# Scores of twelve later attention units computed in the first six steps of a fused top-k attention and MLP kernel

## The chip, the cores and the metric

The kernel runs on one core of one Trainium2 chip. The metric is the device time of the program in microseconds (us). All data are 32-bit floats. The core's engines run side by side, each with an instruction queue of its own that it works off in order: TensorE (PE; its weight loads are shown apart as PEld), VectorE (DVE), ScalarE (ACT), GpSimd (POOL) and SyncE (SP), which issues the DMAs here.

## The reference, cut to what matters

```python
def _attn_ref(q, k, v):                       # (8, 8, 576, 64) each
    scores = scale * np.matmul(q, k.transpose(0, 1, 3, 2))
    kth = np.partition(scores, -32, axis=-1)[..., -32:-31]
    scores = np.where(scores >= kth, scores, -1e9)
    attn = np.exp(scores - np.max(scores, axis=-1, keepdims=True))
    attn = attn / (np.sum(attn, axis=-1, keepdims=True) + 1e-09)
    return np.matmul(attn, v)

x = attn_out.transpose(0, 2, 1, 3).reshape(4608, 512)
h = x @ w_in                                  # 512 x 2048
out = np.maximum(0.01 * h, h) @ w_out         # 2048 x 512
```

For each query only its 32 largest scores of 576 stay in the softmax. The output of the eight heads, side by side, then goes through a two-layer MLP with a leaky ReLU.

## The kernel before, in words

**Units.** The 64 (batch, head) combinations are taken as 32 pairs of heads; a pair's q and k lie in tiles of 128 partitions (64 for each head) by 576. A *unit* is 128 query rows of one pair (two heads), or 64 rows of each of two pairs where 576 leaves a remainder. There are 144 units, 18 to a batch: 16 whole and 2 left ones, the left ones first in odd batches.

**A step of the loop (L540) per unit.** The order of all instructions is written out by hand in this loop. Step `s` touches several units at once:

- `top_k` of unit `s` (`cur`) on VectorE: a maximum and a minimum of the two halves (L251), then four rounds of MAX8 (L256) and MATCH_REPLACE8 (L259).
- `mask` of unit `s-1` (`old`) on GpSimd (L269, L270), its exponentials and their sums on ScalarE (`exponents` L273, `sums` L278, which writes `ze`).
- of unit `s-2` (`older`): the reciprocal `rz` on VectorE (L282), the normalization on ScalarE (L285), and the transposition. ScalarE splits each 32-bit word in two halves (L294), SP writes them to DRAM (L295), and a transposing DMA brings them back as the tile `wT` (L299). Units 14, 15, 23 and 31 (`HASTY`) are transposed on TensorE instead.
- `values` of a pair of units whose `wT` has come (L336, TensorE), kept in `x` by ScalarE (`keep_values` L350). For units from 14 on this happens at the end of the even step three after the pair's odd unit, for units 15, 23 and 31 (`HURRIED`) one step sooner. Earlier units take place `MIDDLE`, one step later.
- in every even step, at its end, `scores` of units `s+2` and `s+3`: eight matmuls (L220) into one `narrow` and two `wide` PSUM tiles, then four ScalarE copies (L227) to the tiles `s_sb` (five buffers). The first two units are scored before the loop by `first_scores` (L236, L242), whose shape is two halves of 288 keys for each head.

**The MLP** works on chunks of tokens: two of 128, then seventeen of 256. A chunk becomes ready when the last of its units is in `x`. Its matmuls (`ph` L392, ScalarE's activation into `gT` L398, `pz` L404, copy L413, store L414) are cut into pieces, which `mlp_steps` places between the pieces of attention at seven slots a step. `slot_budget` spreads the work in hand evenly up to the step in which the next chunk becomes ready.

**Before the loop** the two weight matrices come in 16 pieces as 64-bit numbers in the `raw` tiles (three buffers) and are rounded to 32 bits on VectorE, ScalarE, GpSimd and TensorE (`round_weights`).

**Loads.** `load_qk` (L161) issues q and k of a pair on SP, one after the other; five pairs lie in `loads` tiles, and the last three of each round of eight pairs in a `raw` tile. `load_more` runs at the end of each step; a pair's tiles are loaded anew 8 steps after the last unit that uses them. `load_v` does the same for v. SP takes all DMAs in the order of the program: a transfer that has to wait holds those behind it.

**Constants.** `EARLY_SHARE` is the MLP budget of a slot while only the first two chunks are in hand. `HURRY` is 20: before it, normalization is placed later in the step.

## Time and profile before

| quantity | value |
|---|---|
| time of three runs | 1466.9, 1467.38, 1470.24 us; median 1467.38 |
| the profiled execution's own time | 1466.93 us |
| its span | 1465.2 us, granted TensorE clock 0.98 of full |
| TensorE matmul busy | 1395.2 us (95%) |
| VectorE busy | 1320.3 us (90%) |
| ScalarE, GpSimd busy | 1100.4 and 1097.0 us (75% each) |
| a step of VectorE with no wait in it | 8.87 us on the mean of two (17.7 us for a pair of steps) |
| first `top_k` starts | 60.9 us |
| DMAs | 222.30 MB, 152 GB/s over the span |
| landing of a DMA after its issue, median | 2.1 us for 288 KB of `split`, 3.2 and 3.7 us for q and k (288 KB), 6.7 us for 1024 KB of weights |

How to read it: the page of the profile gives the busy time of each engine and 40 equal slices of the span; a digit is the busy share of one slice (36.6 us) in tenths. The chain of waits goes back from the last instruction, at each step to what released it. In a timeline or a group list, the square bracket or the last column gives the idle time of the engine just before an instruction, and who ended it. A record such as `L220 ... x8` counts matmul records, and a 32-bit matmul leaves two of them. Idle time of an engine that is not the bound costs nothing.

### The profile page before, as it was taken

Reading aid. Unit: us, or ns where it says so; the run is one execution under the profiler, and the core shown is the slowest. Engines: PE = TensorE matmul, PEld = TensorE weight load, DVE = VectorE, ACT = ScalarE, POOL = GpSimd, SP = SyncE. Lnnn points to the kernel's source line nnn. Section 1 sums busy time; section 2 is a strip of 40 time slices with the busy share of each in tenths; the row PEclk is TensorE's granted clock in tenths of the full one; section 3 lists DMA queues with packets and bytes.
Section 4 is the critical chain, followed back from the end, with each engine's and each line's share of the span. In section 5 each row is a group of like instructions: output and inputs, shape, how many; then the busy total and the mean of one; then the engine's idle time right before and its main releaser. Section 6 shows DMA issues by size and latency. Waiting matters only on the chain.

```text
span 1465.2 us, 24106 instructions
## 1 busy us (share of the span) xinstructions
PE 1395.2 (95%) x8066; PEld 927.8 (63%) x8068; DVE 1320.3 (90%) x3401; ACT 1100.4 (75%) x1984; POOL 1097.0 (75%) x744
## 2 busy tenths in 40 slices
PE   7617999999999999999999999999999999999999
PEld 2314548575757676767676767666666666666674
DVE  7999999999999999999999999999999999999600
ACT  8658878777887777777777777777777777777710
POOL 3388888878888888787878888878788878787700
PEclk9957999999999999999999999999999999999999
DMA  9834534654366455665567545655467555664510
GB/s 329 304 85 133 146 105 116 171 154 136 107 196 185 129 137 155 171 185 137 146 168 193 141 138 132 194 174 148 128 167 202 136 140 144 155 141 132 148 45 14
DMA packets 388940, 222.30 MB, mean 152 GB/s; under 512 B 333904, under 2 KB 333904, under 8 KB 386896
## 3 DMA queue, kind: packets, MB, share of 16 engines
q1 hardware_dynamic: 388816, 220.77, 53.7%
q8 instruction: 63, 1.03, 0.3%
q14 instruction: 61, 0.50, 0.1%
HBM read 46.14 MB, written 92.01 MB: 94 GB/s over the span
## 4 chain that ended last, share of the span: by engine, by line
PE 81%; DVE 16%; ACT 1%; issue 1%; DMA 0%; POOL 0%; DVEq 0%; SPq 0%; ACTq 0%; POOLq 0%
PE pz L404 31%; PE ph L392 30%; PE wide L336 10%; DVE tops L256 6%; PE wide L220 6%; DVE pairs L259 5%; PE narrow L220 3%; DVE pairs L251 2%; DVE w_out L155 1%; DVE scale L152 1%; DVE w_in L155 1%; DMA raw<-in_weights_dram 0%; DVE top L133 0%; DVE scale L131 0%; ACT s_sb L285 0%
## 5 line engine op out<-in xcount | busy, mean ns | idle before, releaser
L269 POOL TENSOR_SCALAR pen<-s_sb,tops 128x576 f32<-128x576 f32 x288 | 637.7, 2214 | 208.7 <-DVE tops L256 144.5
L256 DVE MAX8 tops<-pairs 128x8 f32<-128x288 f32 (+1 forms) x1152 | 635.9, 591 | 0.0
L404 PE MATMUL pz<-w_out,gT 128*128 128x512 f32 x1152 | 505.1, 595 | 2.4 <-ACT scale L365 2.4
L392 PE MATMUL ph<-x,w_in 128*128 128x256 f32 x2176 | 482.9, 381 | 0.9 <-ACT gT L398 0.9
L259 DVE MATCH_REPLACE8 pairs<-tops,pairs 128x288 f32<-128x288 f32 (+1 forms) x864 | 460.2, 538 | 0.0
L392 PEld LDWEIGHTS ph<-x,w_in 128*128 128x128 f32 x2176 | 409.4, 190 | 77.7 <-issue 22.2
L270 POOL TENSOR_TENSOR s_sb<-s_sb,pen 128x576 f32<-128x576 f32 x288 | 406.6, 1412 | 24.0
L404 PEld LDWEIGHTS pz<-w_out,gT 128*128 128x128 f32 x1152 | 216.4, 190 | 267.2 <-issue 262.5
L294 ACT COPY split<-s_sb 128x1152 uint16<-128x1152 uint16 x280 | 309.4, 1146 | 0.0
L285 ACT ACTIVATE s_sb<-s_sb,rz 128x576 f32<-128x576 f32 x288 | 207.6, 773 | 43.4 <-DVE rz L282 43.4
L273 ACT ACTIVATE s_sb<-s_sb,nbias 128x576 f32<-128x576 f32 x288 | 222.3, 772 | 12.8 <-POOL s_sb L270 12.8
L251 DVE TENSOR_TENSOR pairs<-s_sb 128x576 f32<-128x576 f32 x288 | 213.5, 780 | 9.9
L336 PEld LDWEIGHTS wide<-wT,vt 128*64 128x64 f32 x3200 | 161.7, 139 | 65.1 <-issue 34.6
L336 PE MATMUL wide<-wT,vt 128*64 128x128 f32 (+1 forms) x3200 | 179.1, 268 | 22.4 <-ACT s_sb L227 21.1
L398 ACT ACTIVATE gT<-ph 128x512 f32<-128x512 f32 x136 | 80.7, 593 | 56.3 <-PE ph L392 55.6
L227 ACT COPY s_sb<-wide 128x704 f32<-128x704 f32 x142 | 107.2, 755 | 21.0 <-PE wide L220 21.0
L350 ACT COPY x<-wide 128x128 f32<-128x128 f32 (+1 forms) x160 | 32.2, 260 | 112.5 <-PE wide L336 112.4
L220 PE MATMUL wide<-kt,qt 64*128 64x352 f32 (+1 forms) x392 | 76.4, 503 | 26.0 <-ACT s_sb L227 23.0
L413 ACT COPY o_sb<-pz 128x512 f32<-128x512 f32 x36 | 21.1, 586 | 98.0 <-PE pz L404 98.0
L227 ACT COPY s_sb<-narrow 128x448 f32<-128x448 f32 x142 | 68.7, 537 | 1.2 <-PE narrow L220 0.6
L282 DVE RECIPROCAL rz<-ze 128x2 f32<-128x2 f32 x144 | 22.3, 155 | 45.9 <-ACT ze L278 45.8
L259 DVE MATCH_VALUE_LOAD pairs<-tops,pairs 128x8 f32 x864 | 62.6, 72 | 0.0
(61 smaller groups left out, 623.2 us busy)
## 6 DMA issues: line engine op xcount, KB each, us to landing
apart<-split SPq DMA_DIRECT2D x280, 288.0 KB, 2.1
raw<-in_weights_dram SPq DMA_DIRECT2D x15, 1024.0 KB, 6.7
vt<-in_vk_dram SPq DMA_DIRECT2D x32, 320.0 KB, 3.4
out_dram<-o_sb SPq DMA_DIRECT2D x36, 256.0 KB, 2.6
qt<-in_qT_dram SPq DMA_DIRECT2D x20, 288.0 KB, 3.2
kt<-in_kT_dram SPq DMA_DIRECT2D x20, 288.0 KB, 3.7
raw<-in_qT_dram SPq DMA_DIRECT2D x12, 288.0 KB, 3.2
raw<-in_kT_dram SPq DMA_DIRECT2D x12, 288.0 KB, 3.6
```

Of the source, the lines that this page charges most:

```text
L220: nc.tensor.matmul(to[r0:r0 + u.rows, i, :], qt[d, u.q0:u.q0 + u.rows], kt[d, k0:k1], start=True, stop=True)
L251: nc.vector.tensor_tensor(pairs[:, :, n, :], u.both[:, :, 0:HS], u.both[:, :, HS:S], op)
L256: nc.vector.max(out=u.tops[:, i, r, :], in_=rest[i])
L259: nc.vector.match_replace(out=rest[i], in_to_replace=u.tops[:, i, r, :], in_values=rest[i], imm_value=LOWEST)
L269: nc.gpsimd.tensor_scalar(pen, u.s[i], u.tops[:, i, ROUNDS - 1, 7:8], MASKED, ALU.is_lt, ALU.mult)
L270: nc.gpsimd.tensor_tensor(u.s[i], u.s[i], pen, ALU.add)
L273: nc.scalar.activation(u.s[i], u.s[i], AF.Exp, bias=u.nbias[:, i:i + 1], scale=SCALE, accum_out=u.z[:, i:i + 1])
L285: nc.scalar.activation(u.s[i], u.s[i], AF.Copy, bias=0.0, scale=u.rz[:, i:i + 1])
L294: nc.scalar.copy(split, pairs[:, :, h])
L336: nc.tensor.matmul(po[side * D:(side + 1) * D, o, :], vt[:, c, side, :], u.wT[:, c + side * NKC if c + 1 < NKC else c, r:r + n], start=(c ...
L392: nc.tensor.matmul(ph[:, i, 0:n], w_in[c][:, f * P:(f + 1) * P], x[c][:, 0:n], start=(c == 0), stop=(c == HP - 1),)
L404: nc.tensor.matmul(pz[0:m, 0:DMODEL], gT[:, f, r0:r0 + m], w_out[f // 4][:, f % 4, :], start=(f == 0), stop=(f == NFC - 1),)
```

## The change

Twelve units, namely 24, 25, 32, 33, 40, 41, 48, 49, 56, 57, 64 and 65, are no longer scored two steps ahead of their use, in the groups at the ends of steps 22, 30, 38, 46, 54 and 62. Instead:

- Before the loop, `load_early` brings k (whole) and q (128 columns for each unit) of the two pairs concerned into each of the three `raw` tiles.
- At the ends of steps 0 to 5, `score_early` scores 4, 2, 1, 2, 1 and 2 of the units with `keep_scores`, in the shape of `first_scores`. ScalarE copies the scores into one of three parts of `gT`, which the MLP does not use yet, and SP stores them to a DRAM tile `kept`.
- Three steps ahead of its use, each unit's scores are fetched from `kept` into its `s_sb` tile (`fetch_scores`), on SP right after the step's transposing DMA.
- q and k of the later pairs are put on a list `waiting`, and one tensor of it is issued in a step, in the same place after the transposing DMA, when no fetch takes that place. The three pairs whose q and k lie in `raw` tiles in the first round are loaded at the end of step 5 instead of step 0.
- The `at_once` condition takes `HASTY` in place of `HURRIED`, which adds step 16.

```diff
--- before.py
+++ after.py
@@ -63,6 +63,7 @@
     work = ctx.enter_context(tc.tile_pool(name="work", bufs=2))
     small = ctx.enter_context(tc.tile_pool(name="small", bufs=5))
     halves = ctx.enter_context(tc.tile_pool(name="halves", bufs=3, space=bass.MemoryType.DRAM))
+    kept = ctx.enter_context(tc.tile_pool(name="kept", bufs=1, space=bass.MemoryType.DRAM))
     ps_sc = ctx.enter_context(tc.tile_pool(name="ps_sc", bufs=1, space=bass.MemoryType.PSUM))
     ps_ml = ctx.enter_context(tc.tile_pool(name="ps_ml", bufs=2, space=bass.MemoryType.PSUM))
 
@@ -158,16 +159,20 @@
 
     qk_of, v_of = {}, {}
 
-    def load_qk(pi):
+    def load_qk(pi, at_once=True):
         if pi % (LOADED + 3) < LOADED:
             qt = loads.tile([P, S], F32, name="qt")
             kt = loads.tile([P, S], F32, name="kt")
         else:
             raw = raws.tile([P, WCH, 4], U16, name="raw").rearrange("p n w -> p (n w)").bitcast(F32)
             qt, kt = raw[:, 0:S], raw[:, S:2 * S]
-        nc.sync.dma_start(qt, qT[pi])
-        nc.sync.dma_start(kt, kT[pi])
+        waiting.extend([(qt, qT[pi]), (kt, kT[pi])])
         qk_of[pi] = qt, kt
+        if at_once:
+            while waiting:
+                nc.sync.dma_start(*waiting.pop(0))
+
+    waiting = []
 
     def load_v(pi):
         v_of[pi] = loads.tile([P, NKC, 2, D], F32, name="vt", bufs=LOADED_V)
@@ -240,6 +245,46 @@
         u.s = [u.both[:, i, :] for i in range(2)]
         for i in range(2):
             nc.scalar.copy(u.s[i].rearrange("p (h n) -> p h n", h=2), ps[i][:, :, 0:HS])
+
+    early_of = {}
+
+    def load_early(us):
+
+        raw = raws.tile([P, WCH, 4], U16, name="raw").rearrange("p n w -> p (n w)").bitcast(F32)
+        at = 0
+        for pi in sorted({u.pairs[0] for u in us}):
+            kt = raw[:, at:at + S]
+            nc.sync.dma_start(kt, kT[pi])
+            at += S
+            for u in us:
+                if u.pairs[0] == pi:
+                    early_of[u] = raw[:, at:at + P], kt
+                    nc.sync.dma_start(early_of[u][0], qT[pi][:, u.q0:u.q0 + P])
+                    at += P
+
+    kept_of = {}
+
+    def keep_scores(u):
+
+        k = len(kept_of)
+        qt, kt = early_of.pop(u)
+        ps = [ps_sc.tile([P, 2, 512], F32, name="wide", bufs=2) if (2 * k + i) % 3 else
+              ps_sc.tile([P, 2, 512], F32, name="narrow") for i in range(2)]
+        for half in range(2):
+            for i, _, side, _ in u.parts:
+                d = slice(side * D, (side + 1) * D)
+                nc.tensor.matmul(ps[i][:, half, 0:HS], qt[d, :], kt[d, half * HS:(half + 1) * HS],
+                                 start=True, stop=True)
+        both = gT.rearrange("p f n -> p (f n)")[:, k % 3 * 2 * S:(k % 3 + 1) * 2 * S]
+        for i in range(2):
+            nc.scalar.copy(both[:, i * S:(i + 1) * S].rearrange("p (h n) -> p h n", h=2), ps[i][:, :, 0:HS])
+        kept_of[u] = kept.tile([P, 2 * S], F32, name=f"kept{k}")
+        nc.sync.dma_start(kept_of[u], both)
+
+    def fetch_scores(u):
+        u.both = work.tile([P, 2, S], F32, name="s_sb", bufs=5)
+        u.s = [u.both[:, i, :] for i in range(2)]
+        nc.sync.dma_start(u.both.rearrange("p i n -> p (i n)"), kept_of[u])
 
     def top_k(u):
 
@@ -455,6 +500,9 @@
 
     steps = units
 
+    KEPT = (24, 40, 56)
+    EARLY_SCORES = {0: 4, 1: 2, 2: 1, 3: 2, 4: 1, 5: 2}
+
     def unit(n):
         return steps[n] if 0 <= n < len(steps) else None
 
@@ -486,12 +534,31 @@
     with tc.manual_schedule():
         last = {p: n for n, u in enumerate(steps) for p in u.pairs}
 
+        to_keep = [[steps[n] for n in (a, a + 1, a + 8, a + 9)] for a in KEPT]
+        early_units = {u for us in to_keep for u in us}
+        to_load, to_keep = list(to_keep), [u for us in to_keep for u in us]
+        assert all(len(u.pairs) == 1 for u in to_keep)
+
+        def score_early(count):
+
+            for _ in range(min(count, len(to_keep))):
+                keep_scores(to_keep.pop(0))
+                if len(to_keep) % 4 == 0 and to_load:
+                    load_early(to_load.pop(0))
+
         def load_more(s):
 
             for of, load, n, lag in ((v_of, load_v, LOADED_V, LAG + 1), (qk_of, load_qk, LOADED + 3, 8)):
+                if of is qk_of and to_keep:
+                    while len(of) < LOADED:
+                        load(len(of))
+                    continue
                 while len(of) < NPAIR and (len(of) < n or last[len(of) - n] + lag <= s):
-                    load(len(of))
-                    if lag > LAG + 1 and len(of) > n:
+                    if of is v_of or len(of) < n:
+                        load(len(of))
+                    else:
+                        if not waiting:
+                            load(len(of), at_once=False)
                         break
 
 
@@ -513,6 +580,8 @@
                     pass
             if n:
                 load_weights(n + 2)
+            if n >= len(jobs) - 2:
+                load_early(to_load.pop(0))
             if 0 <= n - len(jobs) + HP + 1 < HP:
                 load_qk(n - len(jobs) + HP + 1)
 
@@ -538,6 +607,7 @@
             attended(*place)
 
         for s in range(len(steps) + LAG + 1):
+            assert s < 7 or not to_keep
             cur, old, older, new = unit(s), unit(s - 1), unit(s - 2), ()
             if s % 2 == 0:
                 new = [u for u in steps[s + 2:s + 4] if u]
@@ -559,7 +629,7 @@
                 weights_of(older)
             mlp_steps(budget)
             weighed = values(s, MIDDLE)
-            at_once = s - 2 in HURRIED or any(at == (s, MIDDLE) for at, _ in ready_at)
+            at_once = s - 2 in HASTY or any(at == (s, MIDDLE) for at, _ in ready_at)
             if at_once:
                 keep(weighed, s, MIDDLE)
             slot()
@@ -575,6 +645,10 @@
                 keep_transposed(older) if s - 2 in HASTY else transpose(older, lambda: mlp_steps(budget))
             if not older or s - 2 in HASTY:
                 mlp_steps(budget)
+            if unit(s + 3) in early_units:
+                fetch_scores(unit(s + 3))
+            elif waiting:
+                nc.sync.dma_start(*waiting.pop(0))
             slot()
             slot()
             mlp_steps(budget)
@@ -584,11 +658,14 @@
             mlp_steps(budget)
             if not at_once:
                 keep(weighed, s, MIDDLE)
+            if new and new[0] in early_units:
+                new = ()
             if new and s < HURRY:
                 scores(new)
             keep(values(s, END), s, END)
             if new and s >= HURRY:
                 scores(new)
+            score_early(EARLY_SCORES.get(s, 0))
             budget = slot_budget(s + 1)
             mlp_steps(budget)
             load_more(s)
```

## The prediction, made before the changed kernel was run

> **What bounds the kernel now.** I read the page first (busy shares, slices, chain), then sums over stretches, then the chain in pieces, then each engine's waits over the same stretches, then the timelines. The page, its shares and three slice rows:
>
> ```profile
> PE 1395.2 (95%) x8066; PEld 927.8 (63%) x8068; DVE 1320.3 (90%) x3401; ACT 1100.4 (75%) x1984; POOL 1097.0 (75%) x744
> ...
> PE   7617999999999999999999999999999999999999
> DVE  7999999999999999999999999999999999999600
> ...
> PEclk9957999999999999999999999999999999999999
> ```
>
> TensorE is full from about the sixth slice to the last, VectorE from the second to about 1380 us. The two change places as the bound, and the early TensorE is idle at half clock. Sums over stretches (start:end, length, then busy us of PE, PEld, DVE, ACT, POOL, clock, DMA share, GB/s):
>
> ```profile
> 60.90:113.90 53.00, 15.04 (x104) 10.76 (x100) 52.56 (x137) 29.70 (x52) 38.13 (x27) 0.61 0.38 110
> ...
> 253.00:387.00 134.00, 133.98 (x780) 88.78 (x779) 126.69 (x330) 101.81 (x192) 106.80 (x73) 1.00 0.51 142
> 387.00:462.00 75.00, 74.80 (x418) 50.49 (x417) 74.44 (x199) 59.84 (x111) 63.78 (x43) 1.00 0.66 187
> 462.00:640.00 178.00, 177.16 (x1143) 124.61 (x1144) 172.27 (x446) 142.11 (x264) 145.47 (x99) 1.00 0.56 153
> 640.00:1403.00 763.00, 762.97 (x4466) 516.95 (x4465) 707.26 (x1843) 594.70 (x1087) 605.60 (x404) 1.00 0.57 154
> ```
>
> In the first row (steps 0 to 5) TensorE does 15 us in 53: 38 us are free there, and 23 of ScalarE. VectorE sets the pace; its waits over 61 to 190 us are empty. Over 190 to 387 us it waits 6.5 us in six places, over 387 to 505 nothing, over 505 to 650 us 4.6, then 26.7 up to 1370 us. All are of one kind, the reciprocal waiting for ScalarE's `ze`, which stands in ScalarE's queue behind work that waits for TensorE. So VectorE's waits measure how late TensorE is. The chain of waits says the same: VectorE 61 to 190 us, TensorE 192 to 384, VectorE 384 to 462, TensorE from there to the end. Two places of it:
>
> ```profile
> 305.48 0.79 PE wide L220 x4
> 306.27 0.76 PE narrow L220 x8
> 307.03 0.59 PE wide L220 x4
> ...
> 460.76 0.08 DVE rz L282
> ...
> 461.55 0.76 ACT s_sb L285
> 462.31 0.49 ACT gT L398
> ...
> 462.85 1.99 PE ph L392 x8
> ```
>
> First: a score group of two units costs TensorE 0.79+0.76+0.59 = 2.14 us on the path. Second: at 462 us TensorE waits for VectorE (through ScalarE's queue), so work taken from it shortly before is lost there.
>
> **What the Trainium skill says.** "TensorE: Matmul & The Clock Gate", section "What's actually happening": the idle array runs at half clock. Agrees: values (L336 x40) take 4.45 to 4.53 us at 107 and 125 us, 2.33 on the later chain. "DMA: Bandwidth & Descriptors", section "Queues, rings and completion order": descriptors of one ring start in order. No run here shows a fetch ahead of a split; the loads L168/L169, issued at 461.62 and 462.25 us right after a transposing transfer, are the nearest thing.
>
> **The change, part by part.**
>
> *Removed.* The groups at the ends of steps 22, 30, 38, 46, 54 and 62 leave TensorE and ScalarE; only their eight matmuls and four copies are missing from either queue, nothing else changes places there. TensorE: 6 x 2.14 = 12.8 us. What each is worth depends on who is late. They ran at 268, 343, 415, 486, 560 and 634 us.
> - 268 and 343 us: TensorE stretch. VectorE's waits after them are 2.23 us (step 27), 0.46, 0.66, 0.38 and 2.50 (step 35). Each gives back 2.14: 4.28, leaving some 2 of the 6.2.
> - 415 us: VectorE waits for nothing until 505, and TensorE already waits 0.89 us before 462.85. Worth 0: the wait becomes 3.0.
> - 486, 560, 634 us: after the switch at 462. TensorE gets 6.42 us ahead in all, against 4.6 us of VectorE waits up to 650 and over 0.3 us a step after. At each point the lead not yet turned into vanished VectorE waits is at most 2.5 us, and score groups run 2.7 to 4.4 us after their step's end, 0.6 where TensorE had just waited. So it fits, barely: 6.42.
> Sum 4.28 + 0 + 6.42 = 10.7 us. From there to the end TensorE is full (762.97 of 763), so this reaches the end unchanged.
>
> ScalarE loses 2 x 0.755 + 2 x 0.537 = 2.6 us per group. It stands between the values and the normalization (L285) that starts the next odd unit's transposition, so that chain also moves forward, by about what TensorE does; otherwise TensorE would run into it. At step 47 L285 starts at 490.3 while its reciprocal was done at 487.4: 2.9 us of room for 2.14.
>
> *Added early.* Twelve units in steps 0 to 5 (4, 2, 1, 2, 1, 2), each eight matmul records and two ScalarE copies. The same shape, L236 and L242, took 1.24 us of TensorE at full clock and 1.18 of ScalarE: 12 x 1.24 = 14.9 us, double at half clock (29.8), against 38 free; 14.2 against 23 free on ScalarE. Steps 0 and 1 hide theirs (ScalarE idles 5.45 us before 83.2). In steps 2 to 5 the copies stand ahead of L285, which idles 1.42, 3.56 and 1.42 us before 92.1, 100.9 and 109.8. At half clock a copy also waits for its matmuls, so a unit costs ScalarE 1.2 to about 2.5 us, six units 7 to 15 us, with slack 4 x 8.87 - 24.3 = 11 us and another 3 to 4 us before `ze` is needed. Most likely it is late once, around step 7: 1 us of VectorE on the path; bounds 0 and 7. A gain is excluded: VectorE waits for nothing there.
>
> *Staging in gT and stores.* 576 KB each, three slots. Nearest rows: 288 KB land in 2.1 to 3.7 us, 1024 KB in 6.7, so about 4.6. Only step 0 has four units in a row; its last waits 1 to 4 us for a slot, hidden by ScalarE's idle step 1 (1.9 us busy in 8.8). gT is first written by the MLP after step 7. Cost 0; without that cover, up to 4 us. On SP the stores delay v(2..4) and q,k(4), needed at steps 7 and 16: 0.
>
> *Early loads.* 18 q and k DMAs, six of them (0.4 to 0.6 us each on SP) between those of pairs 2 and 3. Pair 3 lands some 4 to 8 us later than now, with its scores read by VectorE at 87 us: 0. Pairs 5 to 7, issued from 56.9 us now, move to step 5, needed at step 16: 0, but six loads may hold step 6's split by a few us, whose values have over two steps: 0.
>
> *Fetches.* One per step at steps 21/22, 29/30, ... 61/62, two steps before VectorE reads it: 0 for VectorE. On SP each stands behind the transposing transfer and ahead of the next step's two splits and transposition, and holds their data by at most its own 4.6 us. Who waits is TensorE's values. Where the held unit is the even one, a step or more is left. The odd one (fetches of even steps) lands 0.6 to 2.3 us before the values begin in most pairs, and is first read 1.2 us into them. In four of six places the fetch is clear of the next split by over 2 us. Cost 0.5 us in all, bounds 0 and 12 (6 x (4.6 - 1.2 - 1.4)).
>
> *q and k one tensor a step.* The same 64 DMAs, now one at a time after the transposition instead of two; last of a batch at step 50, needed at 52. 0; a small gain is hidden under a full TensorE.
>
> *`at_once` with HASTY.* Adds step 16, where no values fall due: nothing.
>
> **Sum.** -10.7 + 1.0 + 0.5 = -9.2 us. Profiled execution 1466.93 us (span 1465.2 and 1.7 around it): 1457.7. The median of the runs shown is 0.45 above it: 1458.2 us.
>
> **The rivals.**
> - *The lead cannot be kept.* TensorE meets `gT` or the transposed weights after 486 us and waits, as at 462. If three of the five pairs count: 6.4 - 1.5 = 4.9, 1462.5 us; if two, 1464.6. For it: 0.6 us margins; against: pz matmuls follow 486 us and wait for nothing of ScalarE.
> - *The sixth pair counts or the early cost is nil.* 10.7 to 12.8: 1454.5 to 1456.7.
> - *Early copies hold VectorE 3 to 7 us.* 1460.2 to 1464.2.
> - *Fetches delay the odd units in full.* +12 - 10.7 + 1: 1469.7. Against: two loads of the same bytes sit there now without showing.
> - *Slower: TensorE and ScalarE take turns in steps 0 to 5.* Nothing overlaps: 2.5 us of cold matmuls, 1.2 of copies, 0.4 of hand-over, 4.1 us per unit on ScalarE, 49 for twelve. Free are 23.3 us plus 4.5 before `ze`: VectorE stops 21.4 us, all on the path. 1467.4 - 10.7 + 21.4 = 1478 us. It ends slower from 3.2 us a unit. Against: three PSUM tiles let matmuls run ahead of copies.
> - *TensorE was not the bound.* 1467.
>
> **How the numbers follow.** Forecast 0.50, more of it 0.08, lead not kept 0.22, early hold 0.07, fetches 0.05, turns 0.06, no bound 0.02. The forecast's own range is 1456.7 to 1460. Range 1454.5 (all six pairs, no cost) to 1464.2 leaves out some 0.15. About 0.3% (4.4 us: 1463.0 and 1471.8) is what a measurement can tell. Faster: 0.50 + 0.08 + 0.19 + 0.04 = 0.81; same 0.13; slower 0.06.
>
> **What would show it.** VectorE's first unit still starts at 61 us; its waits over 61 to 190 us stay under 2 us; over 190 to 387 they fall from 6.5 to about 2; TensorE waits some 3 us near 458; VectorE's waits of 505 to 650 nearly vanish. Wrong if VectorE waits in steps 3 to 7, if values wait for `wT` at steps 24, 32, 48, 56, 64, or if TensorE idles after 475 us.

## The result and the profile after

| quantity | before | after |
|---|---|---|
| median of 11 runs each | 1467.91 us (1466.07 to 1470.24) | 1464.68 us (1462.85 to 1466.06) |
| ratio after to before, 95% interval | | 0.9978 [0.9969, 0.9986] |
| profiled execution: its time, its span | 1466.93, 1465.2 us | 1463.63, 1461.7 us |
| TensorE matmul busy | 1395.2 us | 1405.5 us |
| VectorE busy | 1320.3 us | 1320.3 us |

The change gains 3.2 us, where 9.2 was forecast; the time lies just above the upper end of the range. The page of the changed kernel: the shares, three slice rows, and the chain's shares.

```profile
PE 1405.5 (96%) x8066; PEld 932.9 (64%) x8068; DVE 1320.3 (90%) x3401; ACT 1100.9 (75%) x1984; POOL 1097.8 (75%) x744
...
PE   7848999999989999999999999999999999999998
...
DVE  7999999999999999999999999999999999999600
...
PEclk9968999999999999999999999999999999999999
...
PE 77%; DVE 13%; ACT 4%; DMA 4%; issue 1%; SPq 0%; POOL 0%; DVEq 0%; ACTq 0%; POOLq 0%
```

The early scores are where they were meant to be: the second to fourth digits of PE rise (from 6, 1 and 7), and no slice of VectorE falls. New is a share of 4% for DMA in the chain, and an 8 in PE's twelfth digit (402 to 439 us). The same sums over stretches as before (start:end, length, busy us of PE, PEld, DVE, ACT, POOL, clock, DMA share, GB/s):

```profile
60.90:113.90 53.00, 30.16 (x156) 18.87 (x154) 52.62 (x137) 38.08 (x68) 37.72 (x27) 0.71 0.70 236
253.00:387.00 134.00, 131.85 (x757) 87.00 (x754) 128.38 (x335) 98.96 (x187) 108.44 (x74) 1.00 0.60 162
387.00:462.00 75.00, 70.75 (x390) 48.01 (x389) 74.11 (x196) 57.75 (x107) 63.85 (x43) 0.98 0.66 186
462.00:640.00 178.00, 178.00 (x1121) 124.85 (x1120) 174.70 (x454) 139.35 (x259) 147.85 (x99) 1.00 0.66 176
640.00:1403.00 763.00, 762.67 (x4500) 517.86 (x4499) 705.53 (x1840) 592.33 (x1083) 604.42 (x404) 1.00 0.58 155
```

In the first row TensorE does 15 us more in 53, and VectorE is as full as before (52.62 against 52.56). In the second and third TensorE, full before, is idle for 2.15 and 4.25 us. TensorE's waits from 250 us on name the cause (what waited for what: us in total, times, longest), which before was one wait of 0.9 us for `gT`:

```profile
PE wide L381 <- DMA wT<-apart: 4.7, 2, 4.2
PE wide L381 <- DMA vt<-in_vk_dram: 2.0, 2, 1.7
```

In the changed kernel the values are L381, the scores L225, the split copies L339 and their DMAs L340, the transposing DMA L344, v L179 and the fetch L287. The values wait for v (1.7 us of it at one place) and for transposed weights at two places. TensorE's timeline of the changed kernel, with the idle time before an instruction in brackets:

```profile
267.58 1.97 PE L381 MATMUL wide<-wT,vt 128*64 128x64 f32 x60
271.25 0.80 PE L381 MATMUL wide<-wT,vt 128*64 128x64 f32 x20 [1.70 <-DMA vt<-in_vk_dram]
...
426.05 1.31 PE L381 MATMUL wide<-wT,vt 128*64 128x128 f32 x20
431.61 2.40 PE L381 MATMUL wide<-wT,vt 128*64 128x128 f32 x20 [4.25 <-DMA wT<-apart]
```

The long idle time has a second price. The 20 records before it took 1.31 us, the 20 of the same shape behind it 2.40: the trace gives TensorE's granted clock as 0.50 from 431.4 to 434.8 us. With the slower scores that follow, this costs some 1.5 us (an estimate from the two timelines: 1.1 and 0.4).

The chain of waits leads from both places back to DMAs on SP:

```profile
264.88 0.56 SPq L287
265.44 0.05 issue
265.49 5.72 DMA vt<-in_vk_dram
271.21 0.04 issue
271.25 0.83 PE wide L381 x20
...
421.36 5.61 DMA apart<-split
426.97 0.02 SPq L344
426.99 0.03 issue
427.02 4.55 DMA wT<-apart
431.57 0.04 issue
431.61 0.48 PE wide L381
```

At 264.88 us a fetch is issued ahead of v, and v lands 5.7 us after its issue (the median of the page is 3.7). At 421 us the second of the two split tiles takes 5.6 us to land. What stood in front of them is seen on SP, first before, then after (the rows up to 418 us belong to unit 36, the later ones to unit 37):

```profile
411.44 1.39 SPq L295 DMA_DIRECT2D apart<-split  x2
415.08 2.45 SPq L299 DMA_TRANSPOSE wT<-apart  x1
...
421.51 1.38 SPq L295 DMA_DIRECT2D apart<-split  x2
424.71 2.29 SPq L299 DMA_TRANSPOSE wT<-apart  x1
```

```profile
410.26 0.53 SPq L287 DMA_DIRECT2D s_sb<-kept  x1
410.85 0.42 SPq L179 DMA_DIRECT2D vt<-in_vk_dram  x1
411.93 1.39 SPq L340 DMA_DIRECT2D apart<-split  x2
417.15 2.53 SPq L344 DMA_TRANSPOSE wT<-apart  x1
419.74 0.57 SPq L287 DMA_DIRECT2D s_sb<-kept  x1
420.36 0.42 SPq L179 DMA_DIRECT2D vt<-in_vk_dram  x1
420.88 0.85 SPq L340 DMA_DIRECT2D apart<-split  x2
427.02 2.49 SPq L344 DMA_TRANSPOSE wT<-apart  x1
```

The transposing DMA goes out when its tiles have landed. For unit 37 that was 3.2 us after their issue before, and is 6.1 us after it now, behind a fetch and a load of v. The first fetch had done the same to unit 36 (3.6 us before, 5.2 now), so that the second fetch went out late, just ahead of unit 37's tiles.

Where the time went is read from the start of VectorE's first instruction of a unit (L251 before, L296 after), run less before, in us, from the profiled executions. A rise is time lost, a fall time gained:

```
unit (its start before, us)   0    8     10    28    36    48    70    136
                            60.9 131.7 149.4 311.5 386.8 493.2 695.7 1305.8
after                       +0.4  +0.4  +2.2  +2.6  +0.5  +1.3  -3.9  -3.6
e1  score groups gone       +0.8  +0.8  +0.8  -1.5  -4.7  -4.7 -11.0  -8.9
e3  early scores alone      +0.6  +0.6  +2.2  +1.1  +1.1  +1.1  +1.1  +2.2
e11 two groups, v earlier   +0.6  +0.6  +0.6  -2.1  -4.9  -4.9  -9.2  -9.4
e12 middle group from 42    +2.0  +2.0  +3.7  +1.4  -0.8  +3.3  -2.2  -1.9
e13 middle group with room  +0.3  +0.3  +1.8  -0.6  -1.9  -2.0  -8.3  -8.1
e14 two groups, from 26     +0.2  +0.2  +0.2  -2.1  -4.7  -4.7  -9.0  -8.7
```

### The profile page after: what moved, and what is told of

It is laid out like the page before. It is cut to its first block, busy times and chain, and to the rows that moved or that the text cites. A ratio compares the mean times of both kernels' runs of the same rounds, so it can differ in the third digit from the quotient of the medians.

```text
span 1461.7 us, 24213 instructions
## 1 busy us (share of the span) xinstructions
PE 1405.5 (96%) x8066; PEld 932.9 (64%) x8068; DVE 1320.3 (90%) x3401; ACT 1100.9 (75%) x1984; POOL 1097.8 (75%) x744
## 4 chain that ended last, share of the span: by engine, by line
PE 77%; DVE 13%; ACT 4%; DMA 4%; issue 1%; SPq 0%; POOL 0%; DVEq 0%; ACTq 0%; POOLq 0%
PE pz L449 30%; PE ph L437 29%; PE wide L381 10%; DVE tops L301 5%; PE wide L225 5%; DVE pairs L304 4%; PE narrow L225 3%; DMA apart<-split 2%; ACT split L339 1%; DVE pairs L296 1%; DMA raw<-in_weights_dram 1%; ACT s_sb L318 1%; ACT s_sb L330 1%; DVE w_out L156 1%; DMA wT<-apart 1%
## 5 line engine op out<-in xcount | busy, mean ns | idle before, releaser
L339 ACT COPY split<-s_sb 128x1152 uint16<-128x1152 uint16 x280 | 309.5, 1146 | 1.7 <-DMA apart<-split 1.7
L296 DVE TENSOR_TENSOR pairs<-s_sb 128x576 f32<-128x576 f32 x288 | 213.6, 780 | 9.5
L381 PEld LDWEIGHTS wide<-wT,vt 128*64 128x64 f32 x3200 | 161.2, 139 | 53.0 <-issue 36.2
L381 PE MATMUL wide<-wT,vt 128*64 128x128 f32 (+1 forms) x3200 | 179.0, 268 | 10.3 <-DMA wT<-apart 4.7
L232 ACT COPY s_sb<-wide 128x704 f32<-128x704 f32 x130 | 98.0, 754 | 20.1 <-PE wide L225 20.1
L225 PE MATMUL wide<-kt,qt 64*128 64x352 f32 (+1 forms) x360 | 70.4, 507 | 1.0 <-ACT s_sb L247 0.7
L232 ACT COPY s_sb<-narrow 128x448 f32<-128x448 f32 x130 | 62.9, 536 | 1.2 <-PE narrow L225 0.6
```

The lines of the kernel that those rows point to most:

```text
L225: nc.tensor.matmul(to[r0:r0 + u.rows, i, :], qt[d, u.q0:u.q0 + u.rows], kt[d, k0:k1], start=True, stop=True)
L296: nc.vector.tensor_tensor(pairs[:, :, n, :], u.both[:, :, 0:HS], u.both[:, :, HS:S], op)
L339: nc.scalar.copy(split, pairs[:, :, h])
L381: nc.tensor.matmul(po[side * D:(side + 1) * D, o, :], vt[:, c, side, :], u.wT[:, c + side * NKC if c + 1 < NKC else c, r:r + n], start=(c ...
```

## The experiments

The kernel before had medians of 1467.8 to 1468.4 us beside these runs. The diffs below are cut to the lines, or the parts of lines, that matter. Idle times are of one profiled execution each.

```
run                              us       ratio to before [95% interval]
e1  e1_matmuls_gone              1458.87  0.9940 [0.9927, 0.9953]
e2  e2_matmuls_gone_fetch        1473.59  1.0036 [1.0023, 1.0049]
e3  e3_early_only                1469.30  1.0006 [1.0000, 1.0013]
e4  e4_qk_one_at_a_time          1468.90  1.0004 [0.9998, 1.0011]
e5  e5_v_ahead_of_fetch          1467.04  0.9996 [0.9989, 1.0002]
e6  e6_units_clear_of_v          1465.01  0.9979 [0.9971, 0.9988]
e7  e7_fetch_on_act_queue        1470.47  1.0018 [1.0010, 1.0025]
e8  e8_no_middle_group           1461.56  0.9959 [0.9947, 0.9971]
e9  e9_clear_of_v_fixed          1459.79  0.9946 [0.9934, 0.9959]
e10 e10_clear_no_step5           1465.21  0.9981 [0.9970, 0.9991]
e11 e11_v_a_step_earlier         1459.17  0.9941 [0.9929, 0.9954]
e12 e12_middle_group_clear_of_v  1463.39  0.9966 [0.9957, 0.9975]
e13 e13_middle_group_with_room   1461.11  0.9953 [0.9941, 0.9966]
e14 e14_two_groups_hold_nothing  1457.59  0.9930 [0.9916, 0.9943]
```

### Each part alone

**e1: the matmuls' removal, with no fetch.** The kernel before, in which the twelve units' score matmuls are left out and ScalarE copies weights into `s_sb` instead. So ScalarE's copies, which the change removes too, stay here.

```diff
+                for i in range(2):
+                    nc.scalar.copy(u.s[i], w_in[i][:, 0:S])
-                scores(new)
+                (copies if new[0] in early_units else scores)(new)
```

> The kernel before, with the six score groups' matmuls left out: the twelve units' s_sb tiles are filled by ScalarE copies from weight tiles instead (so these units' scores are not the reference's), in the same place of ScalarE's queue; nothing early, no store, no fetch. Theory (the removed TensorE time is worth what was forecast, and the loss lies in the transfers and the early part): 8 to 11 us faster than before, TensorE waits only near 430 to 462 us. Rival (the lead cannot be kept, because values wait for a chain that starts at VectorE): 3 to 5 us faster, with TensorE waiting at several places after 475 us.

1458.87 us. By unit 70 the lead is 11.8 us from its own start; between units 48 and 70 the three groups give 6.4, as forecast (6.42). So TensorE's share of the removal was worth what was forecast up to there. TensorE, ahead of its chain, waits 2.1 us for `wT` at 422 us, where this kernel has no fetch at all, and four waits of 0.3 to 0.8 us after unit 70 take some 2 us of the lead back:

```profile
PE wide L343 <- DMA wT<-apart: 4.4, 5, 2.1
```

**e2: removal and fetches, no early scores.** The same units' matmuls and copies are left out; each fetches 576 KB, always the same tile, in the place of its fetch, and q and k are loaded two at a time as before.

```diff
+            if unit(s + 3) in early_units:
+                fetch(unit(s + 3))
+            if new and new[0] in early_units:
+                new = ()
```

> The kernel before without the six score groups (matmuls and copies), and with a fetch of 576 KB for each of the twelve units, at the same places as in the change, from one DRAM tile that holds the scores of the first unit (so twelve units' scores are not the reference's); nothing is scored or stored early, q and k loads as before. Theory (the fetches hold back v and the split data): about 5 to 6 us faster than before, with TensorE waits near 267 us for v and near 425 us for wT as in the change. Rival (fetches cost nothing, the early part costs all): 9 to 11 us faster, as with no fetch.

1473.59 us: slower than before, which neither expectation had, and 14.7 us slower than e1, although ScalarE has fewer copies here. The fetches have eaten the whole gain:

```profile
PE wide L344 <- DMA wT<-apart: 12.7, 8, 5.9
PE wide L344 <- DMA vt<-in_vk_dram: 1.5, 1, 1.5
```

**e3: early scores alone**, stored and never fetched; the groups stay. This adds the work of the change without its gain.

```diff
-            if unit(s + 3) in early_units:
-                fetch_scores(unit(s + 3))
-            elif waiting:
+            if waiting:
-            if new and new[0] in early_units:
-                new = ()
```

> The changed kernel with its early scores and stores, but every unit is scored again in its old place and nothing is fetched, so all the extra work is added and nothing removed. Theory: 2 us slower than before (0.4 at the start, 1.6 of VectorE waiting in step 8). Rival (the early part is hidden and the loss is elsewhere): within 0.5 us of before.

1469.3 us, about 1 more than before (0 to 1.9 by the interval), where 2 were expected: VectorE loses 1.6 us in step 8 and gets part of it back by unit 28. The early part cost about what the prediction had for it, 1.0.

**e4: q and k one tensor a step, alone**, in the kernel before.

```diff
+            if waiting:
+                nc.sync.dma_start(*waiting.pop(0))
```

> The kernel before with only the q and k loads of later pairs issued one tensor a step right after the transposing transfer. Theory: within 0.7 us of before. Rival (one of two loads at the end of a step held the split data before, or the new place holds it more): 1 to 3 us away, in either direction.

1468.9 us, no difference clear of the noise. With the removal right, the early part near its forecast and the loads nothing by themselves, the fetches are left, and e2 shows their loss without the early part.

### What in a fetch costs

**e5: v and then the fetch.** In the changed kernel the fetch moves behind `load_more`, where v is issued.

```diff
             load_more(s)
+            if unit(s + 3) in early_units:
+                fetch_scores(unit(s + 3))
+            elif waiting:
+                nc.sync.dma_start(*waiting.pop(0))
```

> The changed kernel with the fetch (and the q or k tensor) issued at the end of the step, behind that step's v loads instead of ahead of them. Theory (one part of the loss is v waiting behind the fetch, the other is v and fetch together ahead of the next splits): TensorE's wait for v at 269.5 us goes (1.7 us), its wait for wT near 427 us stays at 3 to 5 us; 1 to 2 us faster than the changed kernel. Rival (the order on the queue is of no account, the bytes are): the same time as the changed kernel within 0.7 us.

1467.04 us, 2.4 slower than the changed kernel, where both expectations had it equal or faster. The wait for v is gone, but `wT` is late instead, by 3.9 us at 286, 5.3 at 432 and 2.3 at 512 us. (The profiled execution is some 9 us above the median, so these show the places more than the sizes.) Turning the two round moves the delay.

**e6: units whose fetches meet no v.**

```diff
-    KEPT = (24, 40, 56)
+    KEPT = (26, 56, 72)
```

> The changed kernel with other units kept: 26, 27, 34, 35, 56, 57, 64, 65, 72, 73, 80, 81, whose fetches fall into no step that loads v (v is loaded at the ends of steps 20, 21, 36 to 39, 56, 57, 72 to 75), and none of whose score groups lies in the stretch that VectorE bounds. Theory (a fetch costs next to nothing by itself; it costs where v is loaded in the same step): TensorE waits under 1 us in all after 250 us, 9 to 12 us faster than before. Rival (each fetch costs about 1 us wherever it lies): 4 to 7 us faster than before.

1465.01 us. At unit 70 it is 8.4 us ahead of before, and TensorE has waited for no fetch by more than 0.3 us. Then TensorE stands once for 7 us:

```profile
PE narrow L225 <- DMA kt<-in_kT_dram: 7.0, 1, 7.0
```

This is at 718 us. The fetches of steps 61, 62, 69 and 70 took the places of q and k tensors on the list, and a pair's k, issued at 721 us, came too late. This is a flaw of that choice of units, mended in e9.

**e7: the fetch on ScalarE's DMA queue.**

```diff
-        nc.sync.dma_start(u.both.rearrange("p i n -> p (i n)"), kept_of[u])
+        nc.scalar.dma_start(u.both.rearrange("p i n -> p (i n)"), kept_of[u])
```

> The changed kernel with the twelve fetches issued by ScalarE, right behind the second split copy, so that SP's queue holds none and the bytes take another ring. Theory (SP's order is what holds v and the splits): the v wait at 269.5 us goes and the wait near 427 us is halved; 2 to 4 us faster than the changed kernel. Rival (the 16 DMA engines are the shared thing, whichever queue issues): the same as the changed kernel, or up to 3 us slower, since the fetch now runs beside the same step's own split and transposition.

1470.47 us, 5.8 worse than the changed kernel. A fetch holds transfers without a place in SP's queue: with none on SP, the v issued at 264.5 us landed after 6.5 us, and the split tiles of unit 36 after 7.4. The run moves the fetch to another time as well, beside its own step's split tiles; those of units 21, 29 and 45, a step later, land in 3.2 to 3.4 us again. So why the whole is slower isn't separated into queue and time. The Trainium skill, "DMA: Bandwidth & Descriptors", section "Issuing engines are not separate DMA queues", says that DMAs of every issuing engine run on the same 16 DMA engines and interleave; the trace agrees, and its waits are longer than the changed kernel's:

```profile
PE wide L381 <- DMA wT<-apart: 8.8, 4, 5.4
PE wide L381 <- DMA vt<-in_vk_dram: 3.5, 1, 3.5
```

### Which fetches cost

**e8: without the middle group.**

```diff
-    KEPT = (24, 40, 56)
+    KEPT = (24, 56)
```

> The changed kernel with eight kept units (24, 25, 32, 33, 56, 57, 64, 65): the group 40, 41, 48, 49 is scored in its old place. Theory (that group's score group at 415 us is worth at most 1 us, the one at 486 us 2.1, and its fetches at steps 37 and 38 cost 3 to 4 through the wait near 427 us): 1 to 2 us faster than the changed kernel, though it removes a third less. Rival (the group is worth 2 us or more as it stands): 2 us slower than the changed kernel.

1461.56 us: fewer early scores, and 3.1 us faster. The wait at 428 us is down to 0.1, the one for v (1.7 at 268 us, with 0.7 for `wT` at 286) remains, and VectorE no longer waits in step 8. Here the early scores end in step 3, and the six loads of q and k go out then, at 104 us; which of the two does it isn't separated.

**e9: e6 with its loads mended**; q and k of a pair go out together where the next step fetches.

```diff
-                            load(len(of), at_once=False)
+                            load(len(of), at_once=unit(s + 4) in early_units)
```

> The changed kernel with the twelve units that are kept chosen so that no step that fetches also loads v or stands next to one (units from 26, 56 and 72 instead of 24, 40 and 56), and with q and k of a pair issued together where the next step fetches, so that no fetch takes the place of a tensor that is due. Theory (a fetch costs nothing by itself; it costs where it stands in front of v or of the split tiles, or pushes a q or k out of its step): six groups of 2.1 us each, 12.8 us, less some 1 us for the early scores: about 1456.5 us, ratio near 0.992, and no idle of TensorE over 1 us after 250 us. Rival (every fetch costs some 0.6 us wherever it stands): about 1463 us, no better than the changed kernel. Second rival (what VectorE can give is spent after four groups, and the wait for transposed weights takes the rest): about 1460 us, with idles of TensorE that wait for wT after 460 us.

1459.79 us, 4.9 better than the changed kernel with as many units, but short of the 1456.5: waits for `wT` of 1.4, 0.9 and 1.8 us at 643, 717 and 789 us, as the second rival had them. They belong to units 61, 69 and 77, whose split tiles stand behind a fetch (table below).

**e10: e9 with the early scores done one step sooner.**

```diff
-    EARLY_SCORES = {0: 4, 1: 2, 2: 1, 3: 2, 4: 1, 5: 2}
+    EARLY_SCORES = {0: 5, 1: 3, 2: 1, 3: 2, 4: 1}
```

> The same as the run with the choice of units and the issue of q and k mended, and the early scores finished one step sooner (5, 3, 1, 2, 1 instead of 4, 2, 1, 2, 1, 2), so that q and k of the first pairs are loaded one step sooner too. Theory (the 1.6 us for which VectorE waits in step 8 come from the q and k loads that stand ahead of the split tiles of step 7): this wait is gone, and the time is 0.5 to 1.2 us below the run with only the units mended. Rival (that wait is paid back later in any case, since TensorE has slack again near 270 us): the same time as that run within 0.3 us. Second rival (more early scores in steps 0 and 1 hold ScalarE and VectorE at 61 us): 1 to 2 us longer, with new waits of VectorE before 120 us.

A miss: 1465.21 us, with runs from 1460.3 to 1470.0. VectorE's waits near step 8 grew to 2.9 us: the q and k loads, a step sooner, stand ahead of another pair of split tiles, which take 8.3 us to the transposing DMA. A wait for `wT` at 646 us is 3.7 us, against 1.4 in e9. Why this kernel varies by 10 us is open.

**e11: e8 with v issued earlier.** v of the second batch goes out at the end of step 20, ahead of the fetch of step 21.

```diff
-last[len(of) - n] + lag <= s
+(last[len(of) - n] | 1) + 3 <= s if of is v_of else last[len(of) - n] + lag <= s
```

> The changed kernel without its middle group of four units (units from 24 and 56 only, as in the run without the middle group), and v loaded as soon as the fourth unit back has been multiplied, all four tensors of a batch in two steps at most, so that v of the second batch is issued at the end of step 20, ahead of the fetch of step 21. Theory (the fetch of step 21 costs because it stands ahead of v): the two waits near 268 and 286 us, 1.7 and 0.7 us, are gone, and the time is some 2.3 us below the run without the middle group, near 1459.3 us. Rival (four loads of v in a row and the fetch fill the same DMA engines, so that the wait only moves to wT): a wait for wT of 2 us or more between 265 and 290 us, and 1461.5 us again.

1459.17 us, where 1459.3 was expected, and 2.4 below e8. TensorE waits for neither v nor `wT` any more:

```profile
PE ph L437 <- ACT gT L443: 0.9, 1, 0.9
PE wide L225 <- ACT x L395: 0.2, 1, 0.2
```

**e12: e11 with a middle group two units later**, clear of v.

```diff
-    KEPT = (24, 56)
+    KEPT = (24, 42, 56)
```

> The run with v a step earlier, and the middle group of four units is there again, two units later than in the changed kernel (from 42 instead of 40), so that its fetches fall in steps 39, 40, 47 and 48 and v of the third batch, now issued at the ends of steps 36 and 38, is ahead of them. All twelve units are scored early again, so the q and k loads at the end of step 5 are back. Theory (a fetch costs where it stands with v ahead of the next split tiles, and nothing elsewhere; the pair near 415 us gives nothing and takes nothing; the early scores of step 5 make VectorE wait about 1 to 1.6 us in step 8): 1459.2 plus about 1, so 1460.2 us, 4.5 us below the changed kernel with as many fetches; no idle of TensorE over 1 us between 250 and 460 us. Rival (the middle group's fetches hold the loop of the transposed weights wherever they are, since TensorE and VectorE are both full there): an idle of 2 to 4 us between 420 and 445 us for wT, and 1462.5 to 1464.5 us.

1463.39 us, in the rival's band, and 4.2 above e11. The theory that only fetches beside v cost has fallen. The idle time is of the rival's kind, longer than its 2 to 4 us. TensorE's timeline:

```profile
441.93 1.31 PE L381 MATMUL wide<-wT,vt 128*64 128x128 f32 x20
448.59 2.40 PE L381 MATMUL wide<-wT,vt 128*64 128x128 f32 x20 [5.35 <-DMA wT<-apart]
```

No v is near. The fetch stands 1.1 us ahead of the split tiles of unit 39, with an output store between, whose part isn't separated. The clock is at half again afterwards, here for 6.8 us.

This led to a table for the *odd* units whose split tiles stand behind a fetch (e1 has no fetch and is there for comparison): from their issue to landing, and the *room*, which is the start of the pair's values less the landing of `wT` (both from the traces; negative where the values start first).

```
            issue to landing     room at wT
run   unit  before   in the run  before  in the run  TensorE idle
after  21    3.1       6.3        1.8      -1.7        0.4
after  29    3.1       5.5        2.1      -1.1        0
after  37    3.1       6.1       -1.3      -5.5        4.25
after  45    3.1       4.8        2.2      -1.1        0
after  53    3.2       4.1        2.3       1.2        0
after  61    3.2       4.7        2.3       0.3        0
e1     37    3.1       3.3       -1.3      -3.4        2.1
e9     61    3.2       6.1        2.3      -2.7        1.4
e9     69    3.1       5.7        2.3      -2.1        0.9
e9     77    3.8       5.7        1.6      -3.1        1.8
e12    39    4.0       6.0       -1.4      -6.6        5.35
e13    41    3.6       5.7        1.2      -1.0        0
e13    45    3.1       4.3        2.2      -0.8        0
```

Every landing in these rows that has a fetch ahead is later, by 1.0 to 3.2 us. TensorE's idle time is the overdraft of the room beyond 1.27 us, which is the even unit's half of the values (1.31 us of x20 in the timelines) less the 0.04 us from landing to start: 5.52 - 1.27 = 4.25, 6.62 - 1.27 = 5.35. At units 37 and 39 the whole 1.3 was spent before the change. The fetch isn't all that takes room: in e1 unit 37 loses 2.0 us of it without one, because TensorE, with the group at 415 us gone, comes to the values earlier. So about half of the 4.25 us in the changed kernel is time that the removal had freed and nothing could use, and the other half came with the fetch and v.

**e13: the middle group where the held units have room.** Units 44, 45, 48 and 49 instead; q and k of one pair together at step 40.

```diff
-    KEPT = (24, 42, 56)
+    KEPT = ((24, 8), (44, 4), (56, 8))
-(a, a + 1, a + 8, a + 9)] for a in KEPT]
+(a, a + 1, a + d, a + d + 1)] for a, d in KEPT]
-at_once=False)
+at_once=s == 40)
```

> As the run with v a step earlier and all twelve units, but the middle group is units 44, 45, 48 and 49, whose fetches fall in steps 41, 42, 45 and 46 and hold the odd units 41 and 45; in the kernel before their transposed weights land 1.2 and 2.2 us before the values begin, against 1.3 us after at units 37 and 39. Pair 12's q and k are issued together at the end of step 40. Theory (a fetch holds the next landing by 2 to 3 us everywhere, and only room at the held odd unit decides what it costs): no idle of TensorE over 1 us between 400 and 520 us apart from the known 0.9 near 460; 1459.2 of the run without the middle group, plus 1 to 1.7 for the wait in step 8, less up to 2.1 for the score group near 486 us: 1458.2 to 1460.9 us. Rival (between 400 and 500 us TensorE and VectorE are both full, so that a fetch costs there whatever the room): an idle of 2 to 5 us for wT, and 1462.5 to 1464.5 us as in the run before.

1461.11 us with twelve units and twelve fetches, 3.6 below the changed kernel (0.2 above the expected band). Its waits from 250 us on:

```profile
PE ph L437 <- ACT gT L443: 2.6, 1, 2.6
PE wide L381 <- DMA wT<-apart: 2.3, 5, 0.7
```

No wait for `wT` is over 0.7 us. The one at 458 us for `gT` has grown from 0.9 to 2.6: this fits the score group near 450 us, taken out where VectorE is the bound and so given back. From unit 48 to 70 the three groups give 6.3 us. Against e11, which has no middle group, the run is still 1.9 us slower: room makes this group's fetches cheap, but no run shows that the group pays.

**e14: a first group whose fetches hold no odd unit.** e11 with the first group two units later: its fetches stand ahead of the even units 22 and 30, and units 23 and 31 are transposed on TensorE. The second group's fetches still stand ahead of units 53 and 61, which have room.

```diff
-    KEPT = (24, 56)
+    KEPT = (26, 56)
```

> The run with v a step earlier and two groups of four units, with the first group two units later (26, 27, 34, 35), so that its fetches fall in steps 23, 24, 31 and 32 and stand ahead of the split tiles of units 22 and 30 and of no odd unit's (23 and 31 are turned on TensorE). Theory: nothing is held there, TensorE waits for nothing between 250 and 400 us, and the time is that of the run with units from 24 or up to 1 us below it: 1458.2 to 1459.2 us. Rival (the score groups two steps later find less of VectorE's waits to fill, or the fetches meet the q and k loads that begin at step 24): 1 to 2 us longer, 1460 to 1461 us.

1457.59 us, 10.2 below before with 8 early units, and the lowest median of all (five runs within 1.1 us), 0.6 under the expected band; its interval overlaps e11's, so that it isn't shown to be the faster of the two. The split tiles of units 22 and 30 are held as well (5.7 and 6.4 us to landing), but nothing waits for them:

```profile
PE ph L437 <- ACT gT L443: 0.9, 1, 0.9
PE wide L381 <- DMA wT<-apart: 0.3, 1, 0.3
```

## Why the prediction was wrong

By its own terms, measured with the table of starts (the profiled executions differ by 3.3 us in time):

```
term                      forecast   changed kernel (units)    elsewhere
start of the first step      0        +0.4  (0)                 +0.2 to +2.0 in other runs
early scores                +1.0      +1.7  (8 to 10)           e3 +1.6, about +0.5 after unit 28
groups at 268, 343 us       -4.3      -1.7  (10 to 36)          e1 -5.4, e11 -5.5, e14 -4.9
group at 415 us              0        +0.9  (36 to 48)          e1 0
groups at 486, 560, 634     -6.4      -5.3  (48 to 70)          e1 -6.4, e13 -6.3
fetches                     +0.5      in the rows above         
rest                         0        +0.3  (70 to 136)
sum                         -9.2      -3.6
```

- **The failed step is "Fetches. [...] Cost 0.5 us in all".** It was sized for the common case and not place by place. By the table, the three stretches with fetches gave 6.1 us, where 10.7 was forecast for the removal: a cost of 4.6 us in place of 0.5, and most of the missing 5.6. (Against the 11.8 us of e1 it is 5.7.) Three things in the step did not hold.
  - "In four of six places the fetch is clear of the next split by over 2 us". In the kernel before, 3.5 to 6.3 us lay between the transposing DMA and the next split tiles in those even steps. But the fetch of the odd step held the even unit's split tiles first (landing after 5.2 to 6.6 us, before 3.1 to 4.9), so that the second fetch went out late: the next splits followed it after 0.6 to 1.6 us in all six places.
  - The odd unit "lands 0.6 to 2.3 us before the values begin in most pairs". This was true at 21, 29, 45, 53 and 61, where TensorE stood idle for 0.4 us together. Unit 37 is not one of the most: its tiles landed 1.3 us after the values began before the change, and there TensorE stood idle for 4.25 us, 2.1 of which e1 shows without a fetch.
  - The loads of v that share the place in steps 21, 37 and 38 were left out. v was late by 1.7 us at 269 us, which with the 0.4 cost the first group its 2.1; with v ahead of the fetch (e11) both waits are gone.

  The pieces were in the bounds (0 to 12) and as a rival; the rival's evidence against, that "two loads of the same bytes sit there now without showing", looked at bytes and not at the room of the unit behind them.
- **The worth of the removal was right up to unit 70.** e1 shows the three late groups at 6.4 and nothing at 415; e13 shows 6.3 with fetches. The first two gave 1.2 us more than forecast in e1, and waits after unit 70 took 2.1 back, so that e1 ends 9.5 us ahead where 10.7 was forecast for the whole removal. The rival "the lead cannot be kept" has 1464.6 us for two pairs, next to the measured 1464.68. That is chance: in the changed kernel the three late groups still gave 5.3 us, and TensorE stood idle once after 475 us, for 0.3.
- **"Worth 0" for 415 us** was right for the group (e1) and wrong for the place. TensorE's values of units 40 and 41 began at 464.77 us before and at 467.18 in the changed kernel, 2.4 later: the idle time and the half clock behind it outweigh the 2.1 that the group had freed and the 0.9 that TensorE waited near 462 us before (the forecast wait of 3 us near 458 us is not there). VectorE shows 1.3 of these 2.4 at unit 48. The other 1.1 is what the three groups after it gave less than in e1 and e13, where TensorE and VectorE are within 0.2 us of each other at these places. This is an estimate from the traces; no run separates it.
- **Early scores** cost 1.7 once, where 1.0 was forecast with bounds 0 and 7. Two things were seen together and not separated. ScalarE has a new wait for its split tiles, 0.0 before, since six q and k loads stand ahead of them on SP (the prediction put this at 0). And the values near 130 us, for which ScalarE waited before too (3.0 us), let it go on at 130.9 us, where it was 129.1.

```profile
L339 ACT COPY split<-s_sb 128x1152 uint16<-128x1152 uint16 x280 | 309.5, 1146 | 1.7 <-DMA apart<-split 1.7
```

- **Stores, `gT`, q and k one at a time.** Stores land in 3.2 us and fetches in 4.8 (median of the page; KB each, us to landing), against an estimate of 4.6 for both. e4 bears out the 0 for q and k by themselves. Beside fetches they seem to matter, as e2 and e6 suggest; e2 also lacks the early scores, so that isn't shown by it alone.

```profile
kept<-gT SPq DMA_DIRECT2D x12, 576.0 KB, 3.2
s_sb<-kept SPq DMA_DIRECT2D x12, 576.0 KB, 4.8
```

Of the signs named, VectorE's waits over 190 to 387 us fell from 6.5 to 5.0 and not to 2, and those over 505 to 650 from 4.6 to 1.6, near what was said. Of the signs of being wrong, values waited for `wT` at step 24, by 0.4 us; step 40, where they waited longest, was not on that list.

## What to carry to other kernels

Work moved off a full engine and kept in DRAM comes back as transfers, and each of those has a price of its own: what is issued right behind it, how late that may land, and what else loads in that step. Make the table of room place by place before choosing which units to move; at one place without room (unit 37) TensorE stood for 4.25 us, as long as two groups had freed. What is freed where another engine is the bound (the group at 415 us) is not worth a fetch at all. Fewer moved units in the right places (e14, eight) beat more in the wrong ones.

## What the runs showed of the hardware

In the changed kernel a 576 KB fetch issued 0.6 to 1.6 us ahead, at some places with a load of v, held the landing of two 288 KB transfers of an odd unit by 1.0 to 3.2 us, to between 4.1 and 6.3 us. With the fetches on ScalarE's queue, and at another time in the step, the waits were longer still (e7). In the changed kernel the DMA engines' busy share over 253 to 387 us was 0.60, against 0.51 before: this mean, far from full, did not tell of the wait behind one transfer.

In the traces of all runs, each of TensorE's waits of 2.8 us or more after 250 us (eleven, up to 7.0 us) came with 3.4 or 6.8 us of granted clock 0.50, which began during the wait or up to 1.2 us after its end. Of three waits between 2.1 and 2.6 us two did (e1 and e5, not e13), and of those under 1.9 us none.

The start of the first step differed by up to 1.8 us between the profiled kernels that score early (+0.2 to +2.0).
